# Attention and a gated feed-forward block in one kernel: scores of two units moved one stage ahead, PSUM banks divided anew, one batch's v cast by DMA

## The chip, the cores and the metric

The kernel runs on one core of a Trainium2 chip. The metric is device time in microseconds (us), lower is better. Below, "page" is the profiler's summary of one execution, "trace" the record behind it. The engines are TensorE (PE, with its weight loads as PEld), VectorE (DVE), ScalarE (ACT), GpSimd (POOL) and SyncE (SP). "POOLq", "SPq" and "ACTq" are the instructions with which these engines issue DMAs.

## What is computed

Two blocks in a row. First attention over 8 batches, 8 heads, 576 positions and 64 dimensions per head, with two masks: heads 0 to 3 see the last 32 positions, heads 4 to 7 every fourth of the last 128. Then a feed-forward block over all 4,608 tokens.

```python
scores = scale * np.matmul(q, k.transpose(0, 1, 3, 2))
rel = pos[:, None] - pos[None, :]
mask_plain = (rel >= 0) & (rel < 32)
mask_dil = (rel >= 0) & (rel < 128) & (rel % 4 == 0)
attn = softmax(np.where(masks, scores, -1e9))
x = np.matmul(attn, v)          # to (B * S, H * D) = (4608, 512)
g, val = x @ w_gate, x @ w_val  # (4608, 1536)
out = (gelu(g) * val) @ w_out   # (4608, 512)
```

## The kernel before

Attention works in **units**. A unit is one batch and two heads, so each batch b has four: 4b to 4b + 3. `pair(n)` names the heads: two units of a batch are plain (832 score columns) and two dilated (768). Batches 2 and 3 take the dilated pair first, all others the plain pair. Each step of a unit is one letter in a schedule that is written out by hand as a string: `S` scores (64x64 matmuls on TensorE), `P` exponential from PSUM into SBUF (ScalarE), `M` mask (VectorE), `D` sums (TensorE), `l` and `r` logarithm and exponential that turn the sums into reciprocals (ScalarE), `N` products with v (TensorE), `X` product times reciprocal, written to xT (VectorE). `S4@4+S5@6` emits two units' matmuls interleaved; the number after `@` places them in PSUM (`base_of` and `win`, lines 383 to 400).

The feed-forward block works in **chunks** of 512 tokens, c = 0 to 8. Each chunk has a gate stage (`gate_words`: 96 matmuls of 128x512, L597; twelve blocks `nb`, each with a gate and a value bank; `g` is Gelu on ScalarE, `u` the product on VectorE) and an output stage (`out_words`: 48 matmuls of 128x512, L604, four blocks of 128 tokens, each summed over 12 matmuls). A number in a string stands for that many feed-forward matmuls. `e` and `w` store a finished block: read from PSUM by ScalarE (`e`, L615) or by VectorE (`w`, L617), then a DMA that SyncE issues. `E` and `G` load ScalarE's tables.

The output stage of chunk c carries the attention of batch c + 1 between its own matmuls (c = 1 to 6), and the gate stage of chunk c + 1 uses the result. Batches 0 and 1 are done in chunk 0. xT has four tiles, one for each pair of heads; `firsts` says in which order the first 16 gate matmuls read them.

PSUM has eight banks of 512 columns. `gate_banks` gives a block's two banks in the gate stage, `out_banks` the bank of each block in the output stage.

Inputs of batches 2 to 7 come through SyncE: `load_first` brings q and k into `stage` (three buffers, fp32), and GpSimd casts them into `s16`. `load_rest` then issues four DMA transposes into the q and k tile (two of them, used in turn), loads v into `stage` with ten DMAs, and GpSimd copies 16 columns of q (L286) and casts v with two instructions (L248). The word `R` in chunk 2 does `load_rest(3)`, `load_first(4)` and `load_rest(4)` one after the other; `F5 H5` in chunk 3 brings batch 5, and so on. Batches 0 and 1 are brought by GpSimd's own DMAs, which cast on the way (`v_cast`), but for the plain half of v: SyncE loads it, for batch 0 into `stage` for `cast_diag`, which spreads it block-diagonally into `vdiag` (L255), for batch 1 once the first block of `wo` has landed (`gate["dma"] = wo[0]`).

At the start GpSimd issues its DMAs and casts in one order: `load_w(0)`, `cast_diag(0)`, `load_w(1)`, `cast_diag(1)`, `load_w(2)`, then in `second` the rest of the weights, batch 1's q and k, `wo` and batch 1's v. `load_w(i)` is one DMA for `wg` and one for `wv` (L153).

Of the kernel before, what the change touches and what calls it, by code (L numbers as in the profile page):

```python
# [21 lines left out]
def kernel(  # L22
# [10 lines left out]
    nc = tc.nc  # L33
    B, H, S, D = q.shape
    NT, DM = out.shape
    DFF = moe_w_gate.shape[1]
    P = 128
# [6 lines left out]
    NCH = NT // CH  # L44
    NNB = DFF // P
# [6 lines left out]
    NB2 = S // BK  # L52
# [95 lines left out]
    def load_w(*parts):  # L148

        for i in parts:  # L150
            for t, w in ((wg_t, moe_w_gate), (wv_t, moe_w_val)):
                src = w[:, WC[i][0] : WC[i][1]].rearrange("(kc p) n -> p kc n", p=P)
                nc.gpsimd.dma_start(out=t[i], in_=src)  # L153
# [24 lines left out]
    def views(b):  # L178

        halves = [qraw[b % 2][:, t * QK : (t + 1) * QK] for t in range(2)]  # L180
        qp, kp = (t[:, 0:1280].rearrange("p (g c) -> p g c", g=2) for t in halves)
        qd, kd = (t[:, 1280:QK].rearrange("p (g r i) -> p g r i", g=2, r=4) for t in halves)
        vp, vd = (vraw[b % 3][:, a : a + 2 * NB2 * D].rearrange("p (e d) -> p e d", d=D) for a in (0, 2 * NB2 * D))
        return qp, qd, kp, kd, vp, vd
# [12 lines left out]
    def st_of(i):  # L197
        return stage[:, 1280 * i : 1280 * i + 1280]
# [29 lines left out]
    def load_v(b, i, plain):  # L228

        st = st_of(i)  # L230
        for g in range(2 * plain):
            for x in range(2):
                rows_ = v[b, 2 * g + x].rearrange("(j p) d -> p j d", p=64)
                dst = st[half_of(x, b and g), 576 * g : 576 * g + 576].rearrange("p (j d) -> p j d", j=NB2)
                gated(nc.sync.dma_start(out=dst, in_=rows_))  # L235
        for g in range(2 - 2 * plain):
            for x in range(2):
                half = st[half_of(x, g), 576 * g : 576 * g + 512]
                rows_ = v[b, HK + 2 * g + x, 0 : 4 * P].rearrange("(i p r) d -> p i (r d)", i=2, r=4)
                nc.sync.dma_start(out=half.rearrange("p (i c) -> p i c", i=2), in_=rows_)  # L240
        for x in range(2 - 2 * plain):
            dst = st[half_of(x), 512:1152].rearrange("p (g c) -> p g c", c=64)[:, 0:10:9]
            heads = slice(HK + 1, HK + 3) if x else slice(HK, HK + 4, 3)
            nc.sync.dma_start(out=dst, in_=v[b, heads, S - 64 : S].rearrange("g p d -> p g d"))

    def cast_v(dst, i):

        nc.gpsimd.tensor_copy(dst, st_of(i)[:, 0:1152].rearrange("p (e d) -> p e d", d=D))  # L248

    def cast_diag(g):  # L250

        st = st_of(0)[:, 0:1152].rearrange("p (e d) -> p e d", d=D)
        at = slice(NB2 * g, NB2 * g + NB2)
        for x in range(2):
            nc.gpsimd.tensor_copy(diag[half_of(x), at, half_of(x)], st[half_of(x), at])  # L255

    def half_of(x, swap=0):
        y = x ^ (1 if swap else 0)
        return slice(64 * y, 64 * y + 64)
# [5 lines left out]
    def turn(dst, src):  # L265
        nc.sync.dma_start_transpose(out=dst, in_=src)
# [11 lines left out]
    def load_rest(b):  # L278
        qp, qd, kp, kd, vp, vd = tiles["two", b] = views(b)
        turn(qp.rearrange("p g (k c) -> p (g k) c", c=P), s16[:, 0:1280])  # L280
        turn(kp.rearrange("p g (k c) -> p (g k) c", c=P), s16[:, 1280:2560])
        turn(qd.rearrange("p g r i -> p (g r) i")[:, :, 0:P], s16[:, 2560:3584])
        turn(kd.rearrange("p g r i -> p (g r) i")[:, :, 0:P], s16[:, 3584:4608])
        for plain in (0, 1):
            load_v(b, 2 - plain, plain)
        nc.gpsimd.tensor_copy(qd[:, :, :, P:NCL], qp[:, :, S:640].rearrange("p g (i r) -> p g r i", r=4))  # L286
        cast_v(vd, 2)
        cast_v(vp, 1)

    def v_cast(b, g, rest=False):  # L290

        dst = views(b)[5][:, NB2 * g : NB2 * g + NB2]
        for x in range(2):
            half = half_of(x, b and g)
            nc.gpsimd.dma_start(
                out=dst[half, 0:8].rearrange("p (i r) d -> p i (r d)", r=4),
                in_=v[b, HK + 2 * g + x, 0 : 4 * P].rearrange("(i p r) d -> p i (r d)", i=2, r=4),
            )
            if rest:
                heads = slice(HK + x, H, 2)  # L300
                if b:
                    heads = slice(HK + 1, HK + 3) if x else slice(HK, HK + 4, 3)
                nc.gpsimd.dma_start(
                    out=views(b)[5][half_of(x), NB2 - 1 : 2 * NB2 : NB2],
                    in_=v[b, heads, S - 64 : S].rearrange("g p d -> p g d"),
                )

    def two_masks():
        for x in range(2):
# [12 lines left out]
    def pair(n):  # L322
        return (n + 2 * (n // NHP in (2, 3))) % NHP

    def is_plain(n):
        return pair(n) < NHP // 2
# [54 lines left out]
    def win(n, at):  # L381

        bank, kind = at // 10, at % 10
        return 512 * bank + ((0, 832, 960) if is_plain(n) else (80, 880, 880))[kind]

    def two_blocks(n):

# [4 lines left out]
        second = [(2 * r + 1, 176 * r + BQ, NCL * r + BK, 80) for r in range(4)]  # L392
        return first + second

    def base_of(n, bank):
        return bank * 512 + (32 if is_plain(n) else 64)

    def bias_first(n, bank):

# [260 lines left out]
    for h in range(0, HK, 2):  # L660
        for t, src, eng in ((0, q, nc.sync), (1, k, nc.scalar)):
            first = eng.dma_start(out=first_p[:, t, h : h + 2], in_=rows_in(src[0, h : h + 2], 6))  # L662
# [15 lines left out]
    biases()  # L678
    zero()
    bias_first(0, 4)  # L680
    load_w(0)
    cast_diag(0)
    load_w(1)
    cast_diag(1)
    load_w(2)

    def second():
# [16 lines left out]

    def gate_banks(c, nb):

        if c == 0 and nb < 2:
            return ((4, 5), (6, 7))[nb]
        low = ((0, 1), (6, 7) if c else (2, 3))
        return low[(nb + c) % 2]  # L710

    def gate_list(c):

# [11 lines left out]
    def out_list(c, banks):  # L725
        order = [(tb, fc) for tb in range(4) for fc in range(NNB)]
        if c == 0:
            order[: 3 * NNB] = [(tb, 4 * i + fc) for i, tbs in enumerate((range(3), range(3), (2, 0, 1))) for tb in tbs for fc in range(4)]
        return [lambda tb=tb, fc=fc: ffn2(c, tb, banks[tb], fcs=(fc,)) for tb, fc in order]

    def out_banks(c):
        if c == 0:
            return (0, 1, 2, 0)
        return gate_banks(c, 2) * 2 if c < 7 else (6, 7, 4, 5) if c == 7 else (4, 5, 6, 7)

    def run_program(c, words, mms, banks):

# [45 lines left out]
    def gate_words(c):  # L783

        if c == 0:
            return (
# [4 lines left out]
            )  # L791
        loads = {1: "F3", 2: "R", 3: "F5 H5", 4: "F6 H6", 5: "F7 H7"}.get(c, "")
        rest = " ".join(f"4 g{nb} 4 u{nb}" for nb in range(2, NNB - 1))
        before = f"e3@{c - 1}" if 1 < c < NCH - 1 else ""
        return f"{before} {loads} 8 G {'3 g0 1 u0 3 g1 1 u1' if c == 1 else '2 g0 2 u0 2 g1 2 u1'} {rest} 4 g{NNB - 1} 4" + (f" u{NNB - 1}" if c > 6 else "")

    def out_words(c):

        if c == 0:
            return (  # L800
                "V1 F2 S4@4+S5@6 1 E P4 10 P5 1 M4 S6@4+S7@6 M5 1 P6 6 P7 M6 3 D4@40+D5@60 l4 l5 M7 r4 r5 6 w2@0 4 w0@0 4 "
                "w1@0 H2 D6@52+D7@22 N4@50+N5@20 X4 l7 X5 l6 r6 r7 10 N6@20+N7@40 X6 X7 2 e3@0"
            )
        if c > 6:
            return "12 e0 12 e1 12 e2 12 w3" if c < NCH - 1 else "12 e0 12 e1 12 e2 L"
        i, j, k, l = (NHP * (c + 1) + n for n in range(NHP))
        y, z = (0, 3) if c % 2 else (5, 2)
        return (
            f"1 u11 4 S{i}@{y}+S{j}@{z} E P{i} P{j} M{i} M{j} 7 e0 5 S{k}@{y}+S{l}@{z} D{i}@{y}1+D{j}@{z}1 P{k} P{l} M{k} M{l} "
            f"7 e1 l{i} l{j} r{i} r{j} 10 N{i}@{y}0+N{j}@{z}0 D{k}@{y}2+D{l}@{z}2 X{i} X{j} 2 e2 l{k} l{l} r{k} r{l} "  # L810
            f"10 N{k}@20+N{l}@40 X{k} X{l} 2"
        )

    orders = {
# [4 lines left out]
    }  # L819
    firsts = {c: orders[c if c < 3 else 2 if c == 3 else 3] for c in range(NCH)}  # L820

# [36 lines left out]
```

## Time and profile before

| | |
|---|---|
| median of 3 runs | 330.15 us (328.81 to 330.30) |
| the profiled execution | 330.15 us, of which its span is 328.4 us |
| granted clock of TensorE | 1.000 |
| TensorE busy | 320.2 us, 3191 matmuls |
| ScalarE busy | 169.6 us, 258 instructions |
| VectorE busy | 141.1 us, 208 instructions |
| GpSimd busy | 79.2 us, 126 instructions |
| one 128x512 evaluation: Gelu on ScalarE, product on VectorE | 0.598 us, 0.688 us |
| one store's read: ScalarE, VectorE | 0.598 us, 0.692 us |
| one cast of half a batch's v on GpSimd | 1.180 us |

Times in a trace count from the start of the span. A duration of a matmul is modelled: matmuls overlap, so the distance from one start to the next is the better measure. "Idle before, releaser" is the time in which an engine stood still ahead of an instruction and what ended that. In the chain of waits each step is the work that released the next one. Idle time of an engine off the chain costs nothing by itself.

### The profile page before, as it was taken

The numbers are of one execution on the slowest core, as the hardware profiler recorded it, in microseconds if no ns is written. First come the engines' busy times: TensorE is split into PE (matmuls) and PEld (weight loads), VectorE is DVE, ScalarE is ACT, GpSimd is POOL, SyncE is SP. The second block draws the span as 40 slices with busy tenths as digits, with TensorE's granted clock in tenths as the row PEclk, the third lists the DMA queues.
The fourth block names the chain that finished last, engine by engine and source line by source line (L and its number), as shares of the span: only waits on it lengthen the run. The fifth ranks groups of instructions, "written<-read, shape, count | busy, mean of one in ns | idle before, by whom it ended". The sixth has DMA issues, their size and how long they took to land.

```text
span 328.4 us, 7705 instructions
## 1 busy us (share of the span) xinstructions
PE 320.2 (97%) x3191; PEld 155.7 (47%) x3191; DVE 141.1 (43%) x208; ACT 169.6 (52%) x258; POOL 79.2 (24%) x126
## 2 busy tenths in 40 slices
PE   6899998999999999999999999999999999999995
PEld 4754544444544454445444454445444544444443
DVE  6763645544444344343534344345433354204410
ACT  2563565536763577347733783368435853234321
POOL 8693363402331331242214112311000000000000
PEclk9999999999999999999999999999999999999999
DMA  8999996898797899989979657971000200020002
GB/s 192 186 172 206 205 198 125 253 203 199 179 258 170 161 206 176 265 217 181 239 166 246 149 163 179 246 177 66 32 0 26 75 35 0 0 101 29 0 34 96
DMA packets 106659, 47.70 MB, mean 145 GB/s; under 512 B 83584, under 2 KB 102144, under 8 KB 106624
## 3 DMA queue, kind: packets, MB, share of 16 engines
q1 hardware_dynamic: 96352, 39.47, 52.3%
q0 software_dynamic: 9712, 7.08, 14.2%
q10 hardware_dynamic: 560, 0.66, 0.7%
q8 instruction: 25, 0.41, 0.5%
q14 instruction: 10, 0.08, 0.1%
HBM read 37.75 MB, written 9.44 MB: 144 GB/s over the span
## 4 chain that ended last, share of the span: by engine, by line
PE 83%; DMA 13%; POOL 1%; SPq 1%; issue 0%; DVE 0%; POOLq 0%
PE ps L597 51%; PE ps L604 26%; PE ps L432 5%; DMA wo<-in_moe_w_out_dram 5%; DMA stage<-in_v_dram 5%; DMA wg<-in_moe_w_gate_dram 2%; DMA u_all<-in_q_dram 2%; PE ps L628 1%; SPq L235 1%; POOL vdiag L255 1%; POOL v L248 0%; POOL wv L153 0%; POOL wg L153 0%; SPq L662 0%; DVE osb L637 0%
## 5 line engine op out<-in xcount | busy, mean ns | idle before, releaser
L760 DVE SCALAR_TENSOR_TENSOR u_all<-g,ps 128x512 f16<-128x512 f16 x108 | 74.2, 688 | 105.3 <-PE ps L597 91.8
L755 ACT ACTIVATE g<-ps 128x512 f16<-128x512 f32 x108 | 64.4, 598 | 103.8 <-PE ps L597 103.8
L597 PE MATMUL ps<-xT,wg 128*128 128x512 f16 x432 | 114.7, 379 | 0.1
L597 PE MATMUL ps<-xT,wv 128*128 128x512 f16 x432 | 114.0, 379 | 0.1
L604 PE MATMUL ps<-wo,u_all 128*128 128x512 f16 x420 | 97.0, 380 | 0.0
L597 PEld LDWEIGHTS <-wv 128*128 128x128 f16 x432 | 42.1, 98 | 51.5 <-DMA wv<-in_moe_w_val_dram 0.6
L597 PEld LDWEIGHTS <-wg 128*128 128x128 f16 x432 | 42.1, 98 | 50.6 <-issue 0.2
L604 PEld LDWEIGHTS <-u_all 128*128 128x128 f16 x420 | 38.7, 98 | 44.5 <-issue 0.3
L588 DVE TENSOR_TENSOR xT<-ps,rb 128x576 f16<-128x576 f32 x32 | 28.8, 938 | 27.2 <-PE ps L432 22.1
L462 ACT ACTIVATE P<-ps 128x832 f16<-128x832 f32 (+1 forms) x32 | 25.3, 835 | 15.3 <-PE ps L432 15.3
L248 POOL CAST v<-stage 128x1152 f16<-128x1152 f32 x13 | 15.3, 1180 | 66.1 <-DMA stage<-in_v_dram 66.1
L615 ACT ACTIVATE osb<-ps 128x512 f32<-128x512 f32 x31 | 18.5, 598 | 21.3 <-PE ps L604 21.0
L211 POOL CAST s<-stage 128x640 f16<-128x640 f32 x24 | 17.0, 736 | 40.0 <-DMA stage<-in_q_dram 23.7
L559 ACT ACTIVATE lg<-ps 128x576 f32<-128x576 f32 x30 | 18.2, 650 | 4.9 <-issue 3.0
L565 ACT ACTIVATE rb<-lg 128x576 f32<-128x576 f32 x30 | 19.0, 688 | 0.1
L223 POOL CAST s<-stage 128x512 f16<-128x512 f32 x24 | 14.4, 629 | 11.3 <-DMA stage<-in_q_dram 7.7
L467 DVE TENSOR_TENSOR P<-P,two_p 128x832 f16<-128x832 f16 x14 | 10.5, 755 | 12.8 <-ACT P L462 12.7
L467 DVE TENSOR_TENSOR P<-P,two_d 128x768 f16<-128x768 f16 x14 | 9.3, 676 | 12.5 <-ACT P L462 10.2
L780 ACT ACT_TABLE_LOAD x9 | 11.5, 1283 | 0.2
L432 PEld LDWEIGHTS <-q 64*64 64x64 f16 x576 | 7.7, 107 | 6.7 <-issue 5.1
L432 PEld LDWEIGHTS <-v 64*64 64x64 f16 x600 | 7.4, 107 | 6.7 <-issue 5.1
L432 PE MATMUL ps<-q 64*64 64x96 f16 (+2 forms) x576 | 9.9, 203 | 0.3 <-DVE q L334 0.3
(66 smaller groups left out, 122.4 us busy)
## 6 DMA issues: line engine op xcount, KB each, us to landing
out_dram<-osb SPq DMA_DIRECT2D x35, 256.0 KB, 3.0
stage<-in_v_dram SPq DMA_DIRECT2D x32, 144.0 KB, 3.5
stage<-in_q_dram SPq DMA_DIRECT2D x24, 128.0 KB, 3.5
stage<-in_k_dram SPq DMA_DIRECT2D x24, 128.0 KB, 2.9
stage<-in_q_dram SPq DMA_DIRECT2D x6, 512.0 KB, 4.5
stage<-in_k_dram SPq DMA_DIRECT2D x6, 512.0 KB, 5.4
stage<-in_v_dram SPq DMA_DIRECT2D x24, 128.0 KB, 3.1
wo<-in_moe_w_out_dram POOLq DMA_DIRECT2D x3, 512.0 KB, 16.6
```

Of the source, the lines that this page charges most:

```text
L211: nc.gpsimd.tensor_copy(s16[:, 1280 * t + 640 * g : 1280 * t + 640 * g + 640].rearrange("p (k c) -> p k c", k=5), st_of(i).rearrange("p (k ...
L432: nc.tensor.matmul(o[cols], lhs[rows], rhs[rows], start=st, stop=end, skip_group_check=True)
L462: nc.scalar.activation(pt[:, 0 : src.shape[1]], src, AF.Exp, bias=0.0, scale=scale)
L467: nc.vector.tensor_tensor(pt, pt, mask, ALU.mult)
L559: nc.scalar.activation(lg, psf[:, c0 : c0 + S], AF.Ln)
L565: nc.scalar.activation(rb, tiles.pop(("lg", n)), AF.Exp, scale=-1.0)
L588: nc.vector.tensor_tensor(dst, num, rb, ALU.mult)
L597: nc.tensor.matmul(ps[:, bank, :], w[:, kc, ns], xT[kc][:, tok], start=first, stop=end)
L604: nc.tensor.matmul(ps[:, bank, :], u_all[:, fc, tb * P : (tb + 1) * P], wo_t[fc // 4][:, fc % 4, :], start=(fc == 0), stop=(fc == NNB - 1),)
L615: nc.scalar.activation(osb, ps[:, bank, :], AF.Copy, bias=0.0, scale=1.0 / USCALE)
L755: nc.scalar.activation(g, ps[:, gate_banks(c, args[0])[0], :], AF.Gelu)
L760: nc.vector.scalar_tensor_tensor(u_all[:, nb, :], tiles.pop(("g", nb)), USCALE, val, ALU.mult, ALU.mult)
```

## The change

It has four parts. In the output stages of chunks 2 to 5 the scores of the next batch's first two units (batches 4 to 7) are emitted right behind the last products, at places 12 and 15 in PSUM, and stay there through the next gate stage; the output stages of chunks 3 to 6 begin with `E P P` and have three places with attention matmuls instead of four. Banks: gate stages use 0, 7 and 1, 4 (1, 6 in chunk 1), output stages 0 and 7 in turn, chunks 7 and 8 banks 2, 3, 5, 6. Three of four stores in chunks 1 to 6 change from `e` to `w`. Batch 3's v goes from HBM to its tile by ten casting DMAs of GpSimd. At the start the second pair of weights is issued ahead of the diagonal casts.

```diff
     def load_rest(b):
@@ after the four transposes
-        for plain in (0, 1):
+        by_pool = b == 3
+        if by_pool:
+            v_cast(b, 0, True)
+            v_cast(b, 1)
+            v_cast_plain(b)
+        for plain in range(0 if by_pool else 2):
             load_v(b, 2 - plain, plain)
         nc.gpsimd.tensor_copy(qd[:, :, :, P:NCL], ...)
-        cast_v(vd, 2)
-        cast_v(vp, 1)
+        if not by_pool:
+            cast_v(vd, 2)
+            cast_v(vp, 1)
+    def v_cast_plain(b):
+        for g in range(2):
+            dst = views(b)[4][:, NB2 * g : NB2 * g + NB2]
+            for x in range(2):
+                rows_ = v[b, 2 * g + x].rearrange("(j p) d -> p j d", p=64)
+                nc.gpsimd.dma_start(out=dst[half_of(x, g)], in_=rows_)
...
     def win(n, at):
-        return 512 * bank + ((0, 832, 960) if is_plain(n) else (80, 880, 880))[kind]
+        return 512 * bank + ((0, 832, 960, 0) if is_plain(n) else (80, 880, 880, 64))[kind]
-    def base_of(n, bank):
-        return bank * 512 + (32 if is_plain(n) else 64)
+    def base_of(n, at):
+        return at % 10 * 512 + (32 if is_plain(n) else 64) + 96 * (at // 10)
...
-    load_w(0)
-    cast_diag(0)
-    load_w(1)
-    cast_diag(1)
+    load_w(0, 1)
+    for g in range(2):
+        cast_diag(g)
     load_w(2)
...
     def gate_banks(c, nb):
-        if c == 0 and nb < 2:
-            return ((4, 5), (6, 7))[nb]
-        low = ((0, 1), (6, 7) if c else (2, 3))
-        return low[(nb + c) % 2]
+        if c == 0:
+            return ((4, 5), (6, 7))[nb] if nb < 2 else ((0, 1), (2, 3))[nb % 2]
+        return ((0, 7), (1, 6) if c == 1 else (1, 4))[nb % 2]
     def out_banks(c):
         if c == 0:
-            return (0, 1, 2, 0)
-        return gate_banks(c, 2) * 2 if c < 7 else (6, 7, 4, 5) if c == 7 else (4, 5, 6, 7)
+            return (0, 1, 2, 1)
+        return (0, 7, 0, 7) if c < 7 else (2, 3, 5, 6)
...
     def gate_words(c):
-        before = f"e3@{c - 1}" if 1 < c < NCH - 1 else ""
-        return f"{before} {loads} 8 G {'3 g0 1 u0 3 g1 1 u1' if c == 1 else '2 g0 2 u0 2 g1 2 u1'} {rest} 4 g{NNB - 1} 4" + ...
+        if c == 1:
+            return f"{loads} 8 G 3 g0 1 u0 3 g1 1 u1 {rest} 4 g{NNB - 1} 4"
+        before = f"e3@{c - 1}" if c < NCH - 1 else ""
+        return f"{before} {loads} 7 G 3 g0 1 u0 1 g1 4 u1 {rest} 4 g{NNB - 1} 4" + ...
     def out_words(c):
-        y, z = (0, 3) if c % 2 else (5, 2)
+        first = f"1 u11 4 S{i}@1+S{j}@4 E P{i} P{j} M{i} M{j} 7 w0 5" if c < 3 else f"E P{i} P{j} 1 u11 M{i} M{j} 12 w0 2"
+        after = f"S{l + 1}@12+S{l + 2}@15" if 1 < c < 6 else ""
         return (
-            f"1 u11 4 S{i}@{y}+S{j}@{z} E P{i} P{j} M{i} M{j} 7 e0 5 S{k}@{y}+S{l}@{z} D{i}@{y}1+D{j}@{z}1 P{k} P{l} M{k} M{l} "
-            f"7 e1 l{i} l{j} r{i} r{j} 10 N{i}@{y}0+N{j}@{z}0 D{k}@{y}2+D{l}@{z}2 X{i} X{j} 2 e2 l{k} l{l} r{k} r{l} "
-            f"10 N{k}@20+N{l}@40 X{k} X{l} 2"
+            f"{first} S{k}@1+S{l}@4 D{i}@11+D{j}@41 P{k} P{l} M{k} M{l} "
+            f"{7 if c < 3 else 10} w1 l{i} l{j} r{i} r{j} {10 if c < 3 else 4} N{i}@10+N{j}@40 D{k}@12+D{l}@42 X{i} X{j} "
+            f"{2 if c < 3 else 8} w2 l{k} r{k} l{l} r{l} {8 if c < 3 else 6} N{k}@13+N{l}@43 {after} X{k} X{l} {4 if c < 3 else 5}"
         )
-        2: "002 003 012 013 102 103 112 113 000 001 010 011 100 101 110 111",
-        3: "000 001 010 011 100 101 110 111 002 003 012 013 102 103 112 113",
+        2: "002 003 000 102 103 100 012 013 010 001 011 101 112 113 110 111",
+        3: "000 001 002 100 101 102 010 011 012 003 013 103 110 111 112 113",
```

In chunk 0 the last round of the output blocks runs in the order 2, 1, 0 instead of 2, 0, 1, and block 3 takes bank 1 instead of 0, with `w1@0` ahead of `w0@0`. A word of three digits in the orders is block, gate or value, and xT tile.

More of the change, by code (lines that the diff above doesn't have):

```diff
@@ L727, in out_list @@
         if c == 0:
-            order[: 3 * NNB] = [(tb, 4 * i + fc) for i, tbs in enumerate((range(3), range(3), (2, 0, 1))) for tb in tbs for fc in range(4)]
+            order[: 3 * NNB] = [(tb, 4 * i + fc) for i, tbs in enumerate((range(3), range(3), (2, 1, 0))) for tb in tbs for fc in range(4)]
         return [lambda tb=tb, fc=fc: ffn2(c, tb, banks[tb], fcs=(fc,)) for tb, fc in order]
@@ L793, in gate_words @@
         rest = " ".join(f"4 g{nb} 4 u{nb}" for nb in range(2, NNB - 1))
-        before = f"e3@{c - 1}" if 1 < c < NCH - 1 else ""
-        return f"{before} {loads} 8 G {'3 g0 1 u0 3 g1 1 u1' if c == 1 else '2 g0 2 u0 2 g1 2 u1'} {rest} 4 g{NNB - 1} 4" + (f" u{NNB - 1}" if c > 6 else "")
+        if c == 1:
+            return f"{loads} 8 G 3 g0 1 u0 3 g1 1 u1 {rest} 4 g{NNB - 1} 4"
+        before = f"e3@{c - 1}" if c < NCH - 1 else ""
+        return f"{before} {loads} 7 G 3 g0 1 u0 1 g1 4 u1 {rest} 4 g{NNB - 1} 4" + (f" u{NNB - 1}" if c > 6 else "")
     def out_words(c):
@@ L800, in out_words @@
             return (
-                "V1 F2 S4@4+S5@6 1 E P4 10 P5 1 M4 S6@4+S7@6 M5 1 P6 6 P7 M6 3 D4@40+D5@60 l4 l5 M7 r4 r5 6 w2@0 4 w0@0 4 "
-                "w1@0 H2 D6@52+D7@22 N4@50+N5@20 X4 l7 X5 l6 r6 r7 10 N6@20+N7@40 X6 X7 2 e3@0"
+                "V1 F2 S4@4+S5@6 1 E P4 10 P5 1 M4 S6@4+S7@6 M5 1 P6 6 P7 M6 3 D4@40+D5@60 l4 l5 M7 r4 r5 6 w2@0 4 w1@0 4 "
+                "w0@0 H2 D6@52+D7@22 N4@50+N5@20 X4 l7 X5 l6 r6 r7 10 N6@20+N7@40 X6 X7 2 e3@0"
             )
```

## The prediction

> **What bounds the kernel now.** I read the page first: which engine is full, and what the chain that ended last is made of. Both point at TensorE.
>
> ```profile
> PE 320.2 (97%) x3191; PEld 155.7 (47%) x3191; DVE 141.1 (43%) x208; ACT 169.6 (52%) x258; POOL 79.2 (24%) x126
> ...
> PE 83%; DMA 13%; POOL 1%; SPq 1%; issue 0%; DVE 0%; POOLq 0%
> ```
>
> TensorE (PE) is busy for 97% of the span, at a granted clock of 1.000. The 17% of the chain that are not TensorE must all lie before the steady part. Next I read what TensorE waited for, in the view of waits (us in total, times, longest):
>
> ```profile
> PE ps L645 <- DVE ones L67: 1.5, 1, 1.5
> PE ps L432 <- POOL v L248: 1.1, 1, 1.1
> PE ps L352 <- DMA xT<-in_k_dram: 0.7, 1, 0.7
> ```
>
> These and two shorter waits (0.6 and 0.3) sum to 4.2 us, all of it before 54 us. After that TensorE has nothing named to wait for, so a change of the later chunks can only take away time inside its own stream. The largest wait behind the very start is the 1.1 us for the cast of batch 1's v. The chain, in order of time, tells where that cast comes from:
>
> ```profile
> 14.98 0.66 POOL vdiag L255
> 15.65 0.68 POOL wg L153
> 16.33 0.74 POOL wv L153
> 17.11 0.66 POOL vdiag L255
> 17.83 0.56 POOL vdiag L255
> ...
> 18.44 5.95 DMA wg<-in_moe_w_gate_dram
> 24.68 16.57 DMA wo<-in_moe_w_out_dram
> 43.28 8.70 DMA stage<-in_v_dram
> 52.13 1.16 POOL v L248
> 53.33 0.58 PE ps L432 x40
> ```
>
> Batch 1's v is loaded by SyncE only when the first wo block has landed (41.25), and that block stands in GpSimd's DMA queue behind the weights. So the place of the third weight issue (18.44) on GpSimd sets 53.33.
>
> Last, TensorE's timeline of one output stage (chunk 2, 112.2 to 125.6), to see what a group of attention matmuls costs between the 128x512 ones:
>
> ```profile
> 112.05 1.24 PE L604 MATMUL ps<-wo,u_all 128*128 128x512 f16 x5
> 113.22 0.54 PE L432 MATMUL ps<-q 64*64 64x96 f16 x36
> 113.69 2.76 PE L604 MATMUL ps<-wo,u_all 128*128 128x512 f16 x12
> 116.39 0.56 PE L432 MATMUL ps<-q 64*64 64x96 f16 x36
> 116.78 0.53 PE L432 MATMUL ps<-P,ones 64*64 64x96 f16 x24
> 117.24 3.84 PE L604 MATMUL ps<-wo,u_all 128*128 128x512 f16 x17
> ```
>
> Read the starts, not the modelled durations. A pure gate stage has 96 matmuls in 20.72 us in the chain, 0.216 each. The five output matmuls from 112.05 to 113.22 take 1.17, which is 0.09 over 5 x 0.216; the twelve from 113.69 to 116.39 take 2.70, 0.11 over. So 0.1 us goes whenever the stream turns to 64x64 tiles. The same 36 score matmuls take 0.47 alone (113.22 to 113.69) but 0.39 when another attention group follows (116.39 to 116.78). A separate group thus costs about 0.10 + 0.08 = 0.18 us over a joined one.
>
> **The change part by part.** The sum is made against the profiled execution: 330.15 us with a span of 328.4, so 1.75 lie around the span. 330.15 is also the median of the runs.
>
> 1. Order of weights and diagonal casts on GpSimd. Now the second weight pair is issued behind the first two casts, which wait 0.61 us for v's transfer (landing 14.86). After the change both pairs stand before all four casts. From the rows: the first pair ends 13.60 (12.86 + 0.74), the second 13.60 + 0.74 + 0.75 = 15.09, four casts of 0.66 end 17.73, and the third pair starts about 17.8 instead of 18.44. The wait is covered by the two issues: 0.65 gained. From 24 to 42 us the DMAs move an even 206 GB/s, and between 16 and 18 only 128, so the queue ran thin just ahead of the third pair and what stands behind it should come earlier by all of the 0.65: wo's first block, the v load (its SyncE queue holds nothing else there), its cast, TensorE's group at 53.33. Against it: the first two casts end 16.4 instead of 15.64, and the group that needs them started at 16.13; it comes 0.3 later. That is hidden, because the group at 53.33 waits 1.05 and TensorE's own stream also loses the 0.27 gap that it shows at 26.7 before the second 512-column value weights. Ends: 0 if the queue is full anyway; 1.05 + 0.27 - 0.05, about 1.3, if the v cast stops being the last to come. I take 0.65.
>
> 2. Scores of the first two units of batches 4 to 7. Matmuls are as many as before. In chunks 3 to 6 a separate group of 36 goes; in chunks 2 to 5 the same 36 follow directly on the last product group. So four separate groups fewer: 4 x 0.18 = 0.72. Ends: 4 x 0.10 = 0.4 (the turn alone) and 0.8.
>
> 3. The stores go from ScalarE (0.60 each) to VectorE (0.69 each), three in each of six stages. Neither is the bound: VectorE's 43% become about 47%. In chunks 3 to 6 I placed every wait on the rows of chunk 4 (its output stage starts 180.65). The closest are: the early units' masks end 184.15, needed 184.4; the second unit's logarithm, which waits for VectorE's second product (about 190.25), ends 191.4, needed after 192.1; VectorE's product of the third unit ends 193.8, needed by the third matmul of the next gate, 194.6. With these covers the cost is nothing; without them, each late 0.1 us costs 0.1 per stage. Where VectorE was late, the matmul that reads the product or overwrites its bank would be next.
>
> 4. In chunks 1 and 2 the last product group comes after 8 output matmuls instead of 10, that is 0.43 us earlier, and ScalarE's order becomes log, exp, log, exp. The rows of chunk 2 that bear on it:
>
> ```profile
> 122.54 0.60 ACT L615 ACTIVATE osb<-ps 128x512 f32<-128x512 f32 x1 [0.76 <-PE ps L604]
> 123.04 0.65 ACT L559 ACTIVATE lg<-ps 128x576 f32<-128x576 f32 x1
> 123.94 0.65 ACT L559 ACTIVATE lg<-ps 128x576 f32<-128x576 f32 x1 [0.25 <-DVE xT L588]
> ...
> 121.73 2.17 DVE L588 TENSOR_TENSOR xT<-ps,rb 128x576 f16<-128x576 f32 x2 [2.16 <-PE ps L432]
> ```
>
> The first product of VectorE ends 122.81, so the first log runs 122.85 to 123.50, its exponential ends about 124.15, and the second log runs to 124.75. In the built program the last product group waits for this log at its 35th matmul of 40, since both touch one PSUM bank. The group would start at 124.16 (12 output matmuls took 2.69, ten take 2.26) and reach that matmul at 124.57: a wait of 0.2. Behind it stand its last matmuls and the whole stream. Twice 0.2 is 0.4; ends 0 and 0.7. I take 0.35.
>
> 5. The new order of the first gate matmuls asks for the last xT product at the tenth matmul instead of the ninth and tenth together. The gate stages of the chain take 20.79, 20.72, 20.72, 20.86, 20.74, 20.74, 20.72: the 0.14 and 0.02s of the later ones can go. I take 0.2 gained; ends 0 and 0.25.
>
> 6. Batch 3's v. Ten transfers leave SyncE's queue and ten of 0.6 us each (those of batch 1: 0.59 to 0.61) enter GpSimd's; two casts of 1.15 go. This matters for batch 4's q and k, now needed at about 124.7, a whole gate stage earlier. Their first two transposes were issued at 116.54 and 119.24 and landed 5.6 later, so the second at 124.8: just too late. Without the ten v transfers (99.70 to 106.30 on SyncE) they move up by some 6 us, and the earlier loads find free stage buffers, as batch 3's v no longer stands in them. On GpSimd ten issues from 94 on end near 101 to 103, past the 97.94 at which batch 3's 16 columns are copied; these are needed at 113.2. So both queues have 6 us or more to spare: cost 0, and 1 to 3 us once if the cover is gone. Batches 5 to 7 have their q at 151, 179 and 212, wanted at about 159, 193 and 227.
>
> The Trainium skill has a rule against part 6. Its page "SBUF — State Buffer", section "SBUF: two separate sides", says that a DMA issued from GpSimd starves while VectorE runs in a two-port mode, and "Who interferes with whom" names tensor_copy and tensor_scalar as such operations; a 620 ns DMA there took 3100. By it, ten issues at 3.1 us would hold GpSimd 25 us longer, batch 4's q would land after 140 and cost TensorE some 16 us, an estimate from that page.
>
> The row decides for me: between 32 and 42 us six such v issues took 0.59 to 0.60 each while VectorE ran its 0.69 us gate products, the same work that runs at 94 to 103.
>
> Sum: -0.65 - 0.72 + 0 + 0.35 - 0.2 + 0 = -1.2, so 330.15 - 1.2 = 328.95, said as 328.9.
>
> **The rivals.** (a) The start is hidden: GpSimd's queue is full anyway and wo lands at 41.25 as before; of the sum -0.55 stays: 329.6. For it: wo's blocks each took 16.6 us, a long queue; against it the dip at 16 to 18. (b) Everything gives its best end: -1.3 - 0.8 - 0.25 + 0 = -2.35: 327.8. For it speaks that VectorE and ScalarE have gaps everywhere; against it the second log of part 4. (c) Slower: VectorE becomes the engine that the last product group waits for. Place: chunks 1 to 6, its two xT products and the logs behind them, with a store of 0.69 put in front. It decides from the point where the second product ends over 0.7 us later than I placed it; then each of six stages waits, 0.6 us if one store more stands ahead: 3.6 - 1.2 = +2.4, or 332.5. For it: parts 3 and 4 leave margins of only 0.3 to 0.8; against it: VectorE was idle 2.7 us ahead of these products in chunk 4. (d) Batch 4's transposes are late (part 6): 1 to 3 us once, 330 to 332. (e) No gain from joined groups, since the 0.08 is only how the rows are cut: 4 x 0.10, 329.2.
>
> **How the numbers follow.** Forecast with (e), 0.55; (a) 0.15; (b) 0.14; (c) 0.10; (d) 0.06. A measurement of this kernel tells about 0.5%, 1.65 us, from no change; its own three runs lie 1.5 apart. Faster by more than that means under 328.5: all of (b) and some 0.22 of the rest, as the forecast lies only 0.45 above that edge: 0.36. Slower means over 331.8: (c) and part of (d), 0.13. The rest, 0.51, is within. The range takes in (b) and (a), and part of (d): 327.2 to 331.0; the forecast's own bounds, from the ends of parts 1 to 5, are 327.8 to 330.4.
>
> **What would show it.** Right: third weight issue near 17.8, wo's first block landing near 40.6, the wait for v at 53 us down to 0.4 or less; three attention groups instead of four in the output stages of chunks 3 to 6, stages there shorter by 0.15 to 0.2 plus the gate's hundredths; a wait of about 0.2 on the log in chunks 1 and 2. Wrong: TensorE waits on VectorE's products or on transposes in any later chunk, GpSimd's ten v issues much over 0.6 us, or a third weight issue that is earlier while wo lands where it did.

## Result and profile after

The changed kernel takes 328.45 us (median of 14 runs, 327.93 to 329.70), the kernel before 330.01 (14 runs, 328.81 to 331.17) beside it: ratio 0.9959, interval 0.9945 to 0.9974. The profiled execution took 328.1 us with a span of 326.4. The forecast was 328.9 and lies inside what repeated runs scatter; most of its terms held, two were off and nearly cancel.

First the page of the changed kernel, busy times and the chain by engine:

```profile
PE 320.4 (98%) x3207; PEld 156.6 (48%) x3207; DVE 150.6 (46%) x226; ACT 159.8 (49%) x240; POOL 83.2 (26%) x134
...
PE 88%; DMA 7%; ACT 2%; DVE 1%; issue 1%; SPq 1%; POOL 0%; ACTq 0%; DVEq 0%
```

TensorE is as busy as before. ScalarE lost 9.8 us and VectorE gained 9.5. The eighteen stores that changed engine (0.60 each on the one, 0.69 on the other) would make 10.8 and 12.4; the rest is other work, such as the plain masks, which took 0.62 each here and 0.76 in the profile of before. New in the chain is ScalarE with 2%. What TensorE waited for (us in total, times, longest) says where it comes in:

```profile
PE ps L659 <- DVE ones L67: 1.5, 1, 1.5
PE ps L446 <- ACT lg L573: 0.5, 2, 0.3
PE ps L611 <- DMA wv<-in_moe_w_val_dram: 0.5, 1, 0.5
```

The wait of 1.1 for batch 1's v is gone, and there are two new ones for a logarithm: the last product groups of chunks 1 and 2. The starts of the gate stages give the account by chunk. Each column is the distance from one gate stage's start to the next; "tail" runs from the last gate stage's start to the end of the span.

| | start of chunk 1 | 1 | 2 | 3 | 4 | 5 | 6 | 7 | tail |
|---|---|---|---|---|---|---|---|---|---|
| before | 57.03 | 34.30 | 34.26 | 34.20 | 34.35 | 34.27 | 34.23 | 31.10 | 34.66 |
| after | 55.53 | 34.69 | 35.10 | 34.02 | 34.03 | 34.02 | 33.63 | 31.08 | 34.30 |
| difference | -1.50 | +0.39 | +0.84 | -0.18 | -0.32 | -0.25 | -0.60 | -0.02 | -0.36 |

Chunk 2 now holds 36 score matmuls more (0.40) and chunk 6 as many fewer; without this move chunk 2 lost 0.44 and chunk 6 gained 0.20. So chunks 3 to 7 gained 0.97, chunks 1 and 2 lost 0.83, the tail gained 0.36. The 1.50 at the start is more than a single pair of profiles can tell, and some 0.15 of the 0.97 is chance too, as the experiments show.

TensorE's timeline of a gaining stage, chunk 4 after:

```profile
180.06 3.40 PE L618 MATMUL ps<-wo,u_all 128*128 128x512 f16 x15
183.40 0.54 PE L446 MATMUL ps<-q 64*64 64x96 f16 x36
183.76 0.56 PE L446 MATMUL ps<-P,ones 64*64 64x96 f16 x28
184.25 3.19 PE L618 MATMUL ps<-wo,u_all 128*128 128x512 f16 x14
187.38 0.58 PE L446 MATMUL ps<-P,v 64*64 64x96 f16 x40
187.79 0.53 PE L446 MATMUL ps<-P,ones 64*64 64x96 f16 x24
188.25 3.19 PE L618 MATMUL ps<-wo,u_all 128*128 128x512 f16 x14
191.38 0.57 PE L446 MATMUL ps<-P,v 64*64 64x96 f16 x44
191.80 0.54 PE L446 MATMUL ps<-q 64*64 64x96 f16 x36
192.28 1.25 PE L618 MATMUL ps<-wo,u_all 128*128 128x512 f16 x5
```

Three places with attention instead of four, and the next batch's scores directly behind the products. There is no gap.

And the losing place, the end of chunk 2, first TensorE, then ScalarE and VectorE:

```profile
120.79 2.33 PE L618 MATMUL ps<-wo,u_all 128*128 128x512 f16 x10
123.05 0.53 PE L446 MATMUL ps<-P,v 64*64 64x96 f16 x34
123.89 0.25 PE L446 MATMUL ps<-P,v 64*64 64x32 f16 x6 [0.31 <-ACT lg L573]
123.95 0.56 PE L446 MATMUL ps<-q 64*64 64x96 f16 x36
...
121.94 0.65 ACT L573 ACTIVATE lg<-ps 128x576 f32<-128x576 f32 x1 [1.89 <-DVE xT L602]
123.21 0.63 ACT L573 ACTIVATE lg<-ps 128x576 f32<-128x576 f32 x1
...
120.72 2.16 DVE L602 TENSOR_TENSOR xT<-ps,rb 128x576 f16<-128x576 f32 x2 [1.67 <-PE ps L446]
```

The 35th product matmul waits until the second logarithm ends at 123.84. The row names 0.31 of idle time, but the group takes 0.90 from its start to the scores behind it, against 0.41 and 0.42 for the groups of 40 and 44 in chunk 4. So the stop cost 0.49 where the row shows 0.31.

### The profile page after: what moved, and what is told of

Same layout as the page of the kernel before. It is cut to its first block, busy times and chain, and to the rows that moved or that the text cites. A ratio compares the mean times of both kernels' runs of the same rounds, so it can differ in the third digit from the quotient of the medians.

```text
span 326.4 us, 7738 instructions
## 1 busy us (share of the span) xinstructions
PE 320.4 (98%) x3207; PEld 156.6 (48%) x3207; DVE 150.6 (46%) x226; ACT 159.8 (49%) x240; POOL 83.2 (26%) x134
## 4 chain that ended last, share of the span: by engine, by line
PE 88%; DMA 7%; ACT 2%; DVE 1%; issue 1%; SPq 1%; POOL 0%; ACTq 0%; DVEq 0%
PE ps L611 55%; PE ps L618 26%; PE ps L446 5%; DMA wv<-in_moe_w_val_dram 3%; DMA stage<-in_v_dram 2%; DMA u_all<-in_q_dram 2%; ACT lg L573 1%; PE ps L642 1%; DVE xT L602 1%; SPq L235 1%; ACT rb L579 1%; PE ps L366 0%; ACT P L476 0%; PE ps L386 0%; POOL wg L153 0%
## 5 line engine op out<-in xcount | busy, mean ns | idle before, releaser
L767 ACT ACTIVATE g<-ps 128x512 f16<-128x512 f32 x108 | 63.6, 597 | 104.8 <-PE ps L611 104.8
L611 PE MATMUL ps<-xT,wg 128*128 128x512 f16 x432 | 113.3, 379 | 0.2
L611 PE MATMUL ps<-xT,wv 128*128 128x512 f16 x432 | 112.8, 379 | 0.5 <-DMA wv<-in_moe_w_val_dram 0.5
L248 POOL CAST v<-stage 128x1152 f16<-128x1152 f32 x11 | 13.2, 1201 | 58.5 <-DMA stage<-in_v_dram 58.5
L631 DVE TENSOR_SCALAR osb<-ps 128x512 f32<-128x512 f32 x22 | 15.1, 687 | 12.8 <-PE ps L618 12.0
L579 ACT ACTIVATE rb<-lg 128x576 f32<-128x576 f32 x30 | 19.7, 691 | 0.5
L629 ACT ACTIVATE osb<-ps 128x512 f32<-128x512 f32 x13 | 7.8, 599 | 22.0 <-PE ps L618 22.0
L481 DVE TENSOR_TENSOR P<-P,two_p 128x832 f16<-128x832 f16 x14 | 8.7, 620 | 9.7 <-ACT P L476 9.5
```

Source lines behind the costliest of these rows:

```text
L481: nc.vector.tensor_tensor(pt, pt, mask, ALU.mult)
L579: nc.scalar.activation(rb, tiles.pop(("lg", n)), AF.Exp, scale=-1.0)
L611: nc.tensor.matmul(ps[:, bank, :], w[:, kc, ns], xT[kc][:, tok], start=first, stop=end)
L631: nc.vector.tensor_scalar(osb, ps[:, bank, :], 1.0 / USCALE, None, ALU.mult)
L767: nc.scalar.activation(g, ps[:, gate_banks(c, args[0])[0], :], AF.Gelu)
```

## The experiments

Part numbers are those of the prediction, 1 to 6. All are timed over five rounds against the kernel before on the same chip; ratios are to it. Four kernels shared a chip in each of the first two sets (before: 329.70 and 329.77), two in the last (before: 329.29).

**Part 1 alone and part 1 undone.** The kernel before with the new order of weights and diagonal casts, and the changed kernel with the old one:

```diff
-    load_w(0)
-    cast_diag(0)
-    load_w(1)
-    cast_diag(1)
+    load_w(0, 1)
+    for g in range(2):
+        cast_diag(g)
     load_w(2)
```

> The kernel before with the new order of weights and diagonal casts alone. Theory (the whole start gain comes from this order): the third weight issue near 17.2, the first wo block lands near 39.5, no wait for v at 53 us, the gate stage of chunk 1 starts at 55.5 to 56.0 instead of 57.19, all later stages as in the kernel before; 1.2 to 1.5 us faster, ratio about 0.996. Rival (half of it is chance: the second k transfer landed at 12.5 in one profile and at 10.9 in the other, with the same instructions ahead of it): gate stage of chunk 1 at 56.3 to 56.7, 0.5 to 0.8 us faster.

> The changed kernel with the old order of weights and diagonal casts. Theory: gate stage of chunk 1 starts at 57.0 to 57.4 as in the kernel before, later stages as in the changed kernel, so 1.2 to 1.5 us slower than the changed one and within 0.5 us of the kernel before, ratio 0.998 to 1.001. Rival (chance): chunk 1 starts at 56.3 or earlier.

The order alone: 328.84, ratio 0.9980 (0.9960 to 1.0001), about 0.66 us, with an interval that just reaches no change. Undone: 329.44, 0.9981 (0.9966 to 0.9997), where the changed kernel had 0.9959 (0.9945 to 0.9974); these intervals overlap. The gate stage of chunk 1 starts at 56.14 with the order alone, between the two ranges, and at 56.33 with it undone, beside the rival's. (The 57.19 for the kernel before is read from the view of the chain; the timeline has 57.03.) The 1.50 of the first pair is thus not the order's alone; by the times, the rival was nearer. Over all profiles of this study the nine with the new order start chunk 1 at 55.34 to 56.80, mean 56.05, the three with the old one at 57.03, 56.33 and 57.03, mean 56.80: 0.75 apart, with ranges that overlap. The rest of the 1.50 was chance. One such thing can be named: in the profile of before the fourth of GpSimd's first transfers, issued at 5.4, landed at about 12.6, and a later issue stood 1.54 us waiting for it; in the profile of after it landed at about 10.7. It is not the only one: with part 6 alone (below) it was on time, and chunk 1 still began at 57.03.

**Chunks 3 to 6 with the string of chunks 1 and 2.** No early scores, four places with attention; the rest of the change stays:

```diff
-        first = f"1 u11 4 S..." if c < 3 else f"E P{i} P{j} 1 u11 M{i} M{j} 12 w0 2"
-        after = f"S{l + 1}@12+S{l + 2}@15" if 1 < c < 6 else ""
+        first = f"1 u11 4 S{i}@1+S{j}@4 E P{i} P{j} M{i} M{j} 7 w0 5"
+        after = ""
...
```

The lines that follow in `out_words` get the numbers of chunks 1 and 2 for all chunks (7, 10, 2, 8, 4).

> The changed kernel without the early scores: chunks 3 to 6 use the string of chunks 1 and 2, four separate attention groups each and 8 output matmuls ahead of the last products. Theory: a separate group costs 0.18, and the wait of 0.3 to 0.45 us for the second logarithm, seen in chunks 1 and 2 of the changed kernel, comes in all six stages, as the second product of VectorE is late everywhere; chunks 3 to 6 take 34.5 to 34.7 each instead of 34.0, 2 us or more slower than the changed kernel, ratio to the kernel before 1.001 to 1.003. Rival (separate groups are free): chunks 3 to 6 differ by the log's wait alone, 34.3 to 34.4.

332.05 us, 1.0064 (1.0042 to 1.0085): over 1% slower than the changed kernel and slower than before. Chunks 3 to 6 take 34.76 to 34.82 instead of 34.02 (33.63 in chunk 6), more than expected, and TensorE waits six times for the logarithm instead of twice:

```profile
PE ps L446 <- ACT lg L573: 1.7, 6, 0.3
```

The last product group of chunk 4, here and then in the kernel before:

```profile
193.81 0.38 PE L446 MATMUL ps<-P,v 64*64 64x96 f16 x18
194.50 0.41 PE L446 MATMUL ps<-P,v 64*64 64x80 f16 x26 [0.32 <-ACT lg L573]
194.84 1.04 PE L618 MATMUL ps<-wo,u_all 128*128 128x512 f16 x4
```

```profile
193.22 0.55 PE L432 MATMUL ps<-P,v 64*64 64x96 f16 x40
193.70 0.60 PE L604 MATMUL ps<-wo,u_all 128*128 128x512 f16 x2
```

It takes 1.03 from its start to the next output matmul, against 0.48: 0.55 lost there. A separate group at 0.18 and this stop give the 0.74 by which chunk 3 is longer; chunks 4 to 6 lose another 0.05 in their gate stages. The new string of chunks 1 and 2, repeated, costs in each stage what it costs there; the early scores are what lets chunks 3 to 6 do without it.

**Ten and two matmuls in chunks 1 and 2.** The distribution of before round the last products, so that the group starts 0.43 later:

```diff
-            f"{2 if c < 3 else 8} w2 l{k} r{k} l{l} r{l} {8 if c < 3 else 6} N{k}@13+N{l}@43 {after} X{k} X{l} {4 if c < 3 else 5}"
+            f"{2 if c < 3 else 8} w2 l{k} r{k} l{l} r{l} {10 if c < 3 else 6} N{k}@13+N{l}@43 {after} X{k} X{l} {2 if c < 3 else 5}"
```

> The changed kernel, with 10 output matmuls ahead of the last product group of chunks 1 and 2 and 2 behind, as in the kernel before. Theory (the products come 0.43 us too early for the log): TensorE waits for no log, chunks 1 and 2 take 34.3 and 34.7 instead of 34.7 and 35.1, 0.8 us faster than the changed kernel, ratio to the kernel before about 0.993. Rival: the products of VectorE come later by as much and the third gate matmul or its bank waits for them instead, no gain.

327.72 us, 0.9930 (0.9904 to 0.9956); chunks 1 and 2 take 34.29 and 34.70, as expected, and no wait for a logarithm is left. The end of its chunk 2:

```profile
121.09 2.76 PE L618 MATMUL ps<-wo,u_all 128*128 128x512 f16 x12
123.79 0.58 PE L446 MATMUL ps<-P,v 64*64 64x96 f16 x40
124.20 0.54 PE L446 MATMUL ps<-q 64*64 64x96 f16 x36
...
123.41 0.63 ACT L573 ACTIVATE lg<-ps 128x576 f32<-128x576 f32 x1
```

The logarithm ends 0.2 later than above (124.04), yet the 35th matmul, near 124.13, finds it done. Part 4 cost 0.40 in each of two stages and bought nothing. Of the rival a little came: the gate stage of chunk 2 takes 20.82 instead of 20.72, with its third matmul 0.10 late, against 0.5 gained in that chunk's output stage. This version was faster than the kernel before. Against the changed kernel the profiles show it 0.8 shorter in chunks 1 and 2, but the ratios (0.9930 here, 0.9966 when it was timed again below, 0.9959 for the changed kernel) do not settle how much of that is kept.

**Batch 3's v again by SyncE and GpSimd's casts**, in the changed kernel (`by_pool = False`), and **part 6 alone**, in the kernel before (`by_pool = b == 3` with `v_cast_plain`):

> The changed kernel with batch 3's v brought as before: ten loads by SyncE and two casts on GpSimd. Two things are to be told apart. (1) The part of the last stage behind TensorE's last matmul: by my theory the end of the program waits for eight groups of DMA semaphores in turn, and where the last store stands among them decides how many waits are left; with ten SyncE DMAs more the last store stands first again, as before the change, so from the start of the last gate stage to the end of the span 34.66 us instead of 34.30. (2) Batch 4's transposes: by my prediction's part 6 they are issued some 6 us later than in the changed kernel, the second one near 118 with a landing near 123 to 124, against a need at about 123.5; TensorE then waits for q in chunk 2 between 0 and 2 us. Theory: median 0.4 to 1.5 us over the changed kernel (328.4), so 328.8 to 330, ratio to the kernel before 0.997 to 1.000, chunk 2 at 35.1 to 36.5. Rival (the cover is not needed and the tail is chance): 328.4, chunk 2 at 35.10, tail 34.30.

> The kernel before with one part of the change alone: batch 3's v by ten casting DMAs of GpSimd. Ten SyncE DMAs fewer, everything else as before. Theory: chunks 1 to 7 stay as they were (34.30, 34.26, 34.20, 34.35, 34.27, 34.23, 31.10, each within 0.05), and from the start of the last gate stage to the end of the span 34.30 instead of 34.66, since the last store comes to stand seventh of eight in the waits at the end instead of first; ratio 0.999. Rival (the tail belongs to the new banks of chunks 7 and 8): tail 34.66, ratio 1.000. By the Trainium skill, page SBUF — State Buffer, the ten issues would take about 3.1 us each; by the rows of the changed kernel 0.6.

With SyncE: 328.70, 0.9971 (0.9960 to 0.9982). Chunk 2 takes 35.00: no wait for q, although the four transposes were issued from 114.72 on instead of 109.49. The first two landed at 122.7 and 123.7, and the scores that read them began at 123.99: 0.3 us of cover instead of about 7.6. So the rival held for the cover, if only just. The tail is 34.7, so my theory held for the tail. Part 6 alone: 329.54, 0.9991 (0.9980 to 1.0002); the chunks as before (34.32, 34.24, 34.21, 34.23, 34.22, 34.23, 31.10) but for chunk 4, 0.12 under the 34.35 of before, and a tail of 34.3, as the theory had it. The 0.12 is not part 6: with the order alone chunk 4 takes 34.23 too. It lies in the gate stage, 20.86 in the profile of before and 20.74 and 20.75 in these two, so it was chance of that one execution.

**Two DMAs more.** The ten-matmul version, in which two stores of chunk 5 are cut in halves:

```diff
-        nc.sync.dma_start(out=out[t0 : t0 + P, :], in_=osb)
+        for cs in (slice(0, 256), slice(256, 512)) if t0 in (2560, 2688) else (slice(0, 512),):
+            nc.sync.dma_start(out=out[t0 : t0 + P, cs], in_=osb[:, cs])
```

> The version with ten and two output matmuls around the last products of chunks 1 and 2, and two stores of chunk 5 cut into two DMAs each (half the columns), so that SyncE issues two DMAs more and nothing else changes. Theory: chunks as in that version (34.29, 34.70, 34.02 four times less 0.4 in the sixth, 31.08) and a tail of 34.66 instead of 34.30: the last store moves from the seventh place among the end's waits to the first. Rival (the tail does not hang on the number of DMAs): 34.30. Time: 327.7 + 0.36 by the theory, near 328.1, ratio 0.994; 327.7 by the rival.

328.39, 0.9955 (0.9940 to 0.9970); tail 34.6. SyncE's waits for the stores at the end, in the order before, after, part 6 alone, v by SyncE, two DMAs more:

```profile
SPq L853 <- DMA out_dram<-osb: 1.8, 1, 1.8
```

```profile
SPq L868 <- DMA out_dram<-osb: 1.4, 2, 1.1
```

```profile
SPq L867 <- DMA out_dram<-osb: 1.4, 2, 1.1
```

```profile
SPq L868 <- DMA out_dram<-osb: 1.8, 1, 1.8
```

```profile
SPq L869 <- DMA out_dram<-osb: 1.7, 1, 1.7
```

Ten SyncE DMAs fewer give the second form, ten more or two more give the first again, whatever else the kernel does. In the built program, the DMAs of SyncE and ScalarE take eight semaphores in turn, and the end waits for these one after the other. Where the last store has the first of them, seven waits come after its landing; where it has the seventh, one does. The traces bear this out: behind the wait that the last landing ends, SyncE's further waits stand 0.06 us apart, seven of them in before and one in after. Six waits of 0.06 are the 0.36. And over all twelve profiles, the four with 217 or 209 such DMAs (one over a multiple of eight) have tails of 34.6 to 34.7, the eight with 207 or 167 (seven over) 34.3.

The 0.7 that this version took more than the ten-matmul one is more than that. Its profiled execution shows a second part: chunk 4 took 34.75 instead of 34.02, away from the edit. That led to the last experiment.

**Stores by ScalarE.** The changed kernel with `e0`, `e1`, `e2` for `w0`, `w1`, `w2` in chunks 1 to 6:

> The changed kernel with the three stores per stage of chunks 1 to 6 read by ScalarE (0.60 us each) instead of VectorE (0.69). Theory (part 3 cost nothing and brought nothing): chunks 3 to 6 stay at 34.0 within 0.1; in chunks 1 and 2 one store's read of 0.60 comes to stand on ScalarE beside the logarithms, so the wait of 0.43 there can grow by up to 0.6 each: 328.4 to 329.6, ratio 0.995 to 0.999. Rival (the stores on VectorE are what makes the shorter stages possible): chunks 3 to 6 grow by 0.2 to 0.6 each, over 329.6. Second rival (VectorE's stores are what makes the logarithms late): the wait for the logarithm goes and chunks 1 and 2 fall to 34.3 and 34.7: 327.7.

333.98 us, 1.0125 (1.0108 to 1.0142). Chunks 3 to 5 take 35.32 instead of 34.02, chunk 6 34.92. The first rival held, with more than its price. The wait and the two groups of chunk 4 that show it:

```profile
PE ps L446 <- ACT lg L573: 4.1, 10, 0.7
...
190.41 0.25 PE L446 MATMUL ps<-P,v 64*64 64x32 f16 x6 [0.23 <-ACT lg L573]
195.11 0.39 PE L446 MATMUL ps<-P,v 64*64 64x80 f16 x25 [0.66 <-ACT lg L573]
```

Each store in front of the logarithms makes both product groups stop: in chunk 4 the places with products take 1.30 and 1.78 us instead of 0.87 and 0.90, 1.31 in all. With the stores at these places in the string, three places instead of four need ScalarE's 0.60 per store elsewhere: part 3 is what makes part 2 pay. Stores by ScalarE put behind the logarithms were not tried.

**All of v by casting DMAs, beside the ten-matmul version once more.** In the execution with two DMAs more, a mask in chunk 4 had taken 1.46 us. The edit is `by_pool = b >= 3`, so that GpSimd casts no v in chunks 2 to 5:

> The version with ten and two output matmuls around the last products of chunks 1 and 2, and part 6 extended: the v of batches 3 to 7, not of batch 3 alone, by casting DMAs of GpSimd, so that the eight casts of 1.15 us on GpSimd go. In the version before it a mask of VectorE took 1.46 us instead of 0.59 where such a cast ran into it, and the stage was 0.73 longer. Theory (these collisions happen by chance in some executions and cost up to 0.7 us each): chunks 3 to 6 at 34.02 and 33.63 with no mask over 1.3 for two after chunk 2, median 0.1 to 0.4 under that of the ten-matmul version measured beside it. The number of SyncE's DMAs falls by 40, which leaves the last store seventh in the waits at the end: tail 34.30. Rival (forty GpSimd issues collide with VectorE's work in their turn): issues over 0.8 us and masks as long as before, no gain or up to 1 us slower.

> The ten-matmul version once more, for the comparison with the version with all of v cast by DMA on the same chip: ratio 0.993 as before (0.9904 to 0.9956), 327.4 to 327.9; a mask lengthened by a GpSimd cast may appear in its profile or not.

All of v by DMA: 327.65, 0.9946 (0.9926 to 0.9966). The ten-matmul version: 328.23, 0.9966 (0.9948 to 0.9983). The medians differ by the 0.1 to 0.4 expected and a little more, but the intervals overlap, so the size is not settled. The profiles tell it in one place. The ten-matmul version's second profile has again a chunk 4 of 34.74, with these rows of GpSimd, VectorE and TensorE:

```profile
182.93 1.15 POOL L248 CAST v<-stage 128x1152 f16<-128x1152 f32 x1 [7.59 <-DMA stage<-in_v_dram]
183.07 1.45 DVE L481 TENSOR_TENSOR P<-P,two_p 128x832 f16<-128x832 f16 x1 [0.16 <-ACT P L476]
184.57 0.57 PE L446 MATMUL ps<-P,ones 64*64 64x96 f16 x26 [0.49 <-DVE P L481]
```

In the changed kernel's profile the two had met the other way round:

```profile
182.96 0.59 DVE L481 TENSOR_TENSOR P<-P,two_p 128x832 f16<-128x832 f16 x1 [0.16 <-ACT P L476]
183.03 1.53 POOL L248 CAST v<-stage 128x1152 f16<-128x1152 f32 x1 [7.83 <-DMA stage<-in_v_dram]
```

In these rows whoever starts first runs on; the other is held until it has ended (the mask ends 0.44 after the cast, the cast 1.01 after the mask). The sums that need the mask follow at 183.76, 0.21 behind its end at 183.55; in the kernel before they had 0.7 (184.67 to 185.38):

```profile
184.08 0.59 DVE L467 TENSOR_TENSOR P<-P,two_p 128x832 f16<-128x832 f16 x1 [0.16 <-ACT P L462]
185.38 0.56 PE L432 MATMUL ps<-P,ones 64*64 64x96 f16 x28
```

The kernel before has such meetings too: in its chunk 5 a mask of 1.28 us beside a cast, which cost it 0.05 at most. So the new string took the cover off this mask, and in some executions the stage loses 0.7: in two of the three profiles of the ten-matmul strings that still cast v on GpSimd, in none of the other profiles with the new string of chunk 4. With all of v by DMA no mask after chunk 2 is longer than 0.59 for one or 1.26 for two, and chunks 3 to 6 are 34.02, 34.02, 34.02 and 33.63. From the start of chunk 1 to the end it takes 270.2 us, the ten-matmul version 270.1 where no cast met the mask and 270.8 where one did.

## Why the prediction was right, and where it was not

1. **Order at the start: right in size, as far as the scatter lets one tell.** Predicted -0.65; the runs with this part alone show -0.66 (interval -1.3 to 0), the profiles' means -0.75. The third weight issue went to 17.2 (17.1 to 17.8 in the nine profiles with the new order; 17.8 said). After's own pair shows -1.50, because its profile had an early start and the profile of before a late one. My rows took one execution's landing times as fixed; they vary by over 1 us. The path was only half right: of the nine profiles with the new order, TensorE waits for v's cast in four, and in five not at all. The chain of after shows that, when v comes in time, the weights hold the start:

```profile
16.56 0.67 POOL vdiag L255
17.22 0.68 POOL wg L153
17.90 8.66 DMA wv<-in_moe_w_val_dram
26.56 0.04 issue
26.61 8.59 PE ps L611 x39
```

The 0.27 gap at this place, which I had counted as going, grew to 0.64 (25.11 to 26.61 for four matmuls that take 0.86), and eight of the nine profiles show a wait for these weights.

2. **Joined groups (part 2): right. The gate's order (part 5): too large.** Predicted -0.72 and -0.20, together -0.92; measured -0.97 over chunks 3 to 7, or -0.81 to -0.86 when the two other profiles with the strings of before (order alone, part 6 alone) are taken for the comparison. By stage, the gate of chunk 4 went from 20.86 to 20.72, the later ones from 20.74 to 20.72. But the two others show 20.74 and 20.75 in chunk 4, so 0.12 of the 0.20 was chance in the one execution that I had read, and what part 5 could gain is below 0.1. The groups make the rest, 0.18 or a little more each. That the whole 0.18 per group came, not 0.10, takes rival (e) away.

3. **Stores on VectorE: right at nothing, wrong in what it is.** It cost nothing, and rival (c), VectorE late, did not come: TensorE waited nowhere for a product. But I had treated the move as a cost to be hidden, when it is the condition of the gain as the string stands: undone, it costs 5.5 us. And of the covers that I listed, the mask's (0.25) was the one that fails, not through stores but through GpSimd's cast; that I had not considered.

4. **The last products of chunks 1 and 2: the step that was mis-sized.** Predicted a wait of 0.2 each, +0.35, at most 0.7; measured 0.39 and 0.44, +0.83 (the profiles with the old order and with v by SyncE have some 0.34 in chunk 2), and the ten-matmul version gives 0.40 each back. The mechanism, the place and the 35th matmul were right. Two things were off. The first logarithm began 1.11 before the product group's start (121.94 to 123.05) where I had put 1.31, so both logarithms came 0.2 later. Half of that is VectorE's first product, which began 0.82 behind the start of the product group that it reads (119.90 to 120.72), not 0.71 (121.02 to 121.73); in the two other profiles it has 0.71 or 0.72 again, so this half was chance. The rest is that I had let it end at half of the row of two and the logarithm follow in 0.04, where the trace has 1.12 for the one product and 0.09 behind it. And the stop costs more than the wait: where I had put 0.2 for both, the rows show 0.20 and 0.31 of idle time, and the groups lost 0.39 and 0.49.

5. **Batch 3's v: right at nothing for the stages, but it gave the tail.** GpSimd's ten issues took near what the row said, six of them 0.60 to 0.65 and the last four 3.03 together, some 0.76 each:

```profile
92.13 0.64 POOL L301 DMA_DIRECT2D v<-in_v_dram  x1
92.77 0.60 POOL L309 DMA_DIRECT2D v<-in_v_dram  x1
93.35 0.61 POOL L301 DMA_DIRECT2D v<-in_v_dram  x1
93.94 0.62 POOL L309 DMA_DIRECT2D v<-in_v_dram  x1
94.52 1.23 POOL L301 DMA_DIRECT2D v<-in_v_dram  x2
95.68 3.03 POOL L320 DMA_DIRECT2D v<-in_v_dram  x4
```

The Trainium skill's rule on starved GpSimd DMAs ("SBUF — State Buffer", "SBUF: two separate sides") speaks of VectorE in a two-port mode, and the slowing to 3.1 is not seen here, nor in the version with all of v by DMA (0.60 to 0.66, the last four of each batch 0.73 to 0.84). Beside the ten issues VectorE ran gate products alone, one input of which is in PSUM, so these rows hardly put that rule to the test; the 16 us that I had estimated by it did not come. Batch 4's transposes went out 7 us earlier than before (109.49 against 116.54; some 6 said). I had called them just too late without this; the run without it showed them just in time, by 0.3 us. The 0.36 of the tail is in no term of the forecast: I had counted the DMAs of part 6 for their queues, not for the end that waits on them.

The sum: -1.2 forecast. Measured -0.7 at the start (runs and means), +0.83, -0.97 and -0.36, together -1.2 again, of which some 0.15 is chance of the profile of before; the medians differ by 1.56 (ratio's interval: 0.9 to 1.8). So the forecast's total owes its place to an unforeseen gain of 0.36 that met a loss 0.48 larger than said. What was not tried alone: the new banks, and part 5 without part 2.

## What to carry to other kernels

When attention matmuls are joined into fewer places, the gain per place is read from the distances between starts, but whether it can be had is decided by the engine that frees the banks: price the work moved off that engine as part of the gain. Before starting a dependent group earlier, follow the last wait in it to its producer's producer, and count a stop inside a group at more than its idle time. Read a term of a few tenths from more than one execution. Judge a start by several profiles, and look at which instructions of other engines lie beside one whose cover shrinks.

## What the runs showed of the hardware

- A cast on GpSimd and a mask multiply on VectorE with both inputs in SBUF exclude each other in the rows shown: 0.59 became 1.45 us, or 1.15 became 1.53, by who began first. The Trainium skill says so ("SBUF — State Buffer", "Who interferes with whom"): a lock held for the whole instruction, not shared bandwidth. These rows agree.
- The place of the last store among the semaphores of the end is worth up to 0.36 us (0.06 per wait behind it), and it shifts with the number of SyncE's and ScalarE's DMAs anywhere in the kernel.
- The same transfer at the start, the fourth that GpSimd issues (at 5.4 us), landed between 10.5 and 12.6 us in different executions; with one and the same order chunk 1 began anywhere from 55.34 to 56.80. What makes it vary was not found.
- A product group stopped at its 35th matmul lost 0.49 us where the row shows 0.31 of idle time, and 0.39 where it shows 0.20; in chunk 4 with the string of chunks 1 and 2 it lost 0.55 where the row shows 0.32.
